# Row sums of q in wide matmuls, with the two half rows joined on ScalarE and VectorE, in an attention and feed-forward kernel

## The chip, the cores and the metric

The kernel runs on one core of a Trainium2 chip. The metric is the device time of one execution in microseconds (us).

Engines: PE is TensorE (PEld its weight loads), DVE is VectorE, ACT is ScalarE, POOL is GpSimd. A load here is a DMA that POOL issues (part 6 of the page lists the loads of k, q and v under POOLq); the profile gives DMA time as a share of 16 DMA engines.

## The reference, cut to what matters

```python
def _attn_ref(q, k, v, tau):                       # B, N, C = 4, 6016, 256
    qn = q / (np.linalg.norm(q, axis=1, keepdims=True) + 1e-06)
    kn = k / (np.linalg.norm(k, axis=1, keepdims=True) + 1e-06)
    s = kn.transpose(0, 2, 1) @ qn / tau           # 256 x 256 per batch
    a = softmax(s)                                 # shortened
    return v @ a
# then a SwiGLU feed-forward over all 24064 rows: (silu(x @ w_gate) * (x @ w_val)) @ w_out
```

The norms are sums of squares over the 6016 rows, for each of the 256 columns. Batch 0 has to be done before the long stretch of dense matmuls can start. Only batch 0's norm of q is touched by the change.

## The kernel before: the parts concerned

q of batch 0 has 47 tiles of 128 rows, taken in 24 pairs. ACT or DVE squares a pair; for pairs 0 to 17 PE sums the squares over the partitions with a matrix of ones, into one row of 256 (`first_row_sums`). The row is copied (`first_row_copy`) and turned into two columns by four PE passes (`first_cols`). The squares of the last pairs are added to these columns directly (`first_col_sums`). The logarithm and exponentials follow.

```python
def first_row_sums(b, t, which, sq, t_last):       # which: 1 for k, 0 for q
    if t == 0:
        ss_new = psum_gv.tile([P, 1 + which, C], FP32, tag="gv"[which])
        state[b, "ss", which] = ss_new
    pm = pairs[t][1]
    ss = state[b, "ss", which]
    if which == 1:                                  # k: one matmul of 512 per pair
        nc.tensor.matmul(ss[:, :pm, :], ones_bf, sq[:, :pm, :], start=(t == 0),
                         stop=(t == t_last), skip_group_check=True)
        return
    for s in range(pm):                             # q: two matmuls of 256 into one row
        nc.tensor.matmul(ss[:, 0, :], ones_bf, sq[:, s, :], start=(t == 0 and s == 0),
                         stop=(t == t_last and s == pm - 1))

def first_row_copy(b):
    row = work.tile([1, C], FP32, tag="row")
    nc.vector.tensor_copy(row, state[b, "ss", 0][0:1, 0, :])
    state[b, "row"] = row
# ...
def keep_warm(n):                                   # dummy matmuls
    ps = psum_o.tile([P, 2, C], FP32, tag="o")
    for _ in range(n):
        nc.tensor.matmul(ps, ones_bf, warm_bf, start=True, stop=True)
# ... order of the loads, all issued by POOL:
#     k, q, then v_sb, then the first two column blocks of w_gate and w_val, ...
# ... in first_softmax, after the column sums:
    rs = psum_m.tile([P, CH], FP32, tag="misc")
    keep_warm(1)
    row_eps(rs)
    transpose_first_v()                             # PE transposes v_sb
    keep_warm(2)
# ... the last pairs of q:
first_row_copy(0)
waiting = []
for n, g in enumerate(range(G_COLS, NQ - 1)):
    ts = range(qgroups[g][0] // 2, (qgroups[g + 1][0] if n < 2 else NS + 1) // 2)
    sqs = [(t, first_square(0, t, 0, on_dve=(t % 2 == 1))) for t in ts]
    for t in ts:
        gemm1_pair(0, t)
    if n == 0:
        first_cols(0)
        keep_warm(1)
    # ... column sums of the group before
```

## Time and profile before

| what | value | read from |
|---|---|---|
| time, first three executions | 809.76, 809.77, 812.23 us | timings |
| span of the profiled one | 808.0 us | page |
| PE busy | 790.9 us, 98% | page, part 1 |
| PE from 35.4 us on | without a hole but 0.10 us at 40.3 and two of 0.07 | table of stretches, PE's timeline |
| start of the dense stretch | first v tile lands at 35.32 | chain of waits |
| first matmul of the output product (o_new) | 52.88 us | PE's timeline |

The page and its views are shown in the prediction below. To read them: busy time is a sum over the whole program; the table of stretches says where PE has holes; the chain of waits, followed back from the end, says which event started the dense stretch. The last row of the table is a ruler: nothing but dense PE work lies between the start of the feed-forward and that matmul, so the time at which it starts tells how late the dense stretch began, holes up to there included.

### The profile page before, as it was taken

Reading aid. Unit: us, or ns where it says so; the run is one execution under the profiler, and the core shown is the slowest. Engines: PE = TensorE matmul, PEld = TensorE weight load, DVE = VectorE, ACT = ScalarE, POOL = GpSimd, SP = SyncE. Lnnn points to the kernel's source line nnn. Section 1 sums busy time; section 2 is a strip of 40 time slices with the busy share of each in tenths; the row PEclk is TensorE's granted clock in tenths of the full one; section 3 lists DMA queues with packets and bytes.
Section 4 is the critical chain, followed back from the end, with each engine's and each line's share of the span. In section 5 each row is a group of like instructions: output and inputs, shape, how many; then the busy total and the mean of one; then the engine's idle time right before and its main releaser. Section 6 shows DMA issues by size and latency. Waiting matters only on the chain.

```text
span 808.0 us, 11840 instructions
## 1 busy us (share of the span) xinstructions
PE 790.9 (98%) x3916; PEld 381.3 (47%) x3916; DVE 554.1 (69%) x856; ACT 454.3 (56%) x802; POOL 249.3 (31%) x299
## 2 busy tenths in 40 slices
PE   4999999999999999999999999999999999999998
PEld 1644444444454444444454444444445444444446
DVE  3777878758667878766766877766866665665654
ACT  3666666555556666555555656555555555555553
POOL 3415887331104786332010768610000000000000
PEclk9999999999999999999999999999999999999999
DMA  8995999899897795877995687556645755555443
GB/s 90 144 158 90 179 158 173 154 114 148 167 147 159 144 154 122 165 122 167 158 175 121 117 157 151 131 131 161 127 118 131 135 133 131 129 145 133 115 112 98
DMA packets 203132, 112.40 MB, mean 139 GB/s; under 512 B 151376, under 2 KB 190160, under 8 KB 202320
## 3 DMA queue, kind: packets, MB, share of 16 engines
q1 hardware_dynamic: 185456, 84.55, 43.7%
q0 software_dynamic: 17472, 27.01, 30.2%
q8 instruction: 30, 0.49, 0.3%
q14 instruction: 30, 0.25, 0.1%
q10 hardware_dynamic: 144, 0.10, 0.0%
HBM read 79.06 MB, written 60.48 MB: 173 GB/s over the span
## 4 chain that ended last, share of the span: by engine, by line
PE 95%; DMA 4%; POOL 0%; issue 0%; DVE 0%; POOLq 0%
PE g_ps L466 30%; PE v_ps L466 30%; PE o_new L507 29%; PE ps L433 2%; DMA q_sb<-in_q_dram 2%; PE kq_new L171 2%; DMA v_sb<-in_v_dram 1%; PE o_new L560 1%; PE last_ps L584 0%; POOL k_sb L114 0%; PE unit_ps L433 0%; PE kq_new L176 0%; PE vt_ps L150 0%; POOL q_sb L114 0%; PE ps L423 0%
## 5 line engine op out<-in xcount | busy, mean ns | idle before, releaser
L476 DVE TENSOR_TENSOR sv<-silu,v_ps 128x512 bf16<-128x512 bf16 (+1 forms) x576 | 386.2, 672 | 214.4 <-ACT silu L472 212.2
L472 ACT ACTIVATE silu<-g_ps 128x512 bf16<-128x512 f32 (+1 forms) x576 | 339.1, 589 | 292.2 <-PE g_ps L466 273.1
L466 PE MATMUL g_ps<-vT,Wg 128*128 128x512 bf16 (+1 forms) x1128 | 330.6, 375 | 0.0
L466 PE MATMUL v_ps<-vT,Wv 128*128 128x512 bf16 (+1 forms) x1128 | 330.4, 374 | 0.0
L507 PE MATMUL o_new<-sv,w_out_sb 128*128 128x512 bf16 (+1 forms) x1104 | 324.5, 376 | 0.0
L466 PEld LDWEIGHTS <-Wv 128*128 128x128 bf16 x1152 | 112.7, 98 | 130.9 <-issue 0.4
L311 POOL TENSOR_TENSOR acc_new<-acc_new,sq 128x512 f32<-128x512 f32 x135 | 157.2, 1164 | 52.3 <-DVE sq L301 36.9
L466 PEld LDWEIGHTS <-Wg 128*128 128x128 bf16 x1152 | 111.3, 98 | 125.7
L507 PEld LDWEIGHTS <-w_out_sb 128*128 128x128 bf16 x1104 | 108.0, 98 | 126.4
L129 POOL DMA_DIRECT2D vb_new<-in_v_dram x47 | 24.2, 515 | 241.5 <-DMA vT<-vb_new 241.0
L517 DVE COPY pl<-o_new 128x512 uint16<-128x512 uint16 (+1 forms) x92 | 62.5, 679 | 14.1 <-ACT pl L516 14.1
L301 DVE TENSOR_TENSOR sq<-q_sb 128x512 bf16<-128x512 fp8e5 x72 | 65.1, 904 | 0.0
L516 ACT COPY pl<-o_new 128x512 uint16<-128x512 uint16 (+1 forms) x92 | 53.1, 577 | 19.6 <-PE o_new L507 19.6
L302 ACT ACTIVATE sq<-k_sb 128x512 bf16<-128x512 fp8e5 x72 | 44.2, 614 | 0.0
L114 POOL DMA_DIRECT2D q_sb<-in_q_dram x45 | 25.4, 566 | 15.3 <-DMA k_sb<-in_k_dram 11.3
L171 PE MATMUL kq_new<-k_sb,q_sb 128*128 128x512 fp8e5 x184 | 28.3, 294 | 0.6 <-DMA q_sb<-in_q_dram 0.6
L171 PEld LDWEIGHTS <-q_sb 128*128 128x256 fp8e5 x184 | 21.1, 136 | 5.0 <-DMA q_sb<-in_q_dram 1.2
L378 POOL TENSOR_SCALAR den<-th 128x512 f32<-128x512 f32 x3 | 1.8, 615 | 66.8 <-ACT th L377 49.8
L114 POOL DMA_DIRECT2D k_sb<-in_k_dram x39 | 21.5, 551 | 1.0 <-POOLq L782 0.8
L346 POOL TENSOR_TENSOR inv<-inv,half 64x8 f32<-64x8 f32 x3 | 5.0, 1665 | 53.3 <-DVE inv L344 53.3
L200 PE MATMUL ss_new<-sq,ones_bf 128*128 128x512 bf16 (+1 forms) x24 | 9.2, 538 | 12.0 <-ACT sq L188 12.0
L306 POOL TENSOR_TENSOR acc_new<-sq 128x512 f32<-128x512 bf16 x3 | 3.5, 1151 | 45.9 <-DVE sq L301 45.9
(94 smaller groups left out, 211.9 us busy)
## 6 DMA issues: line engine op xcount, KB each, us to landing
rows<-pl SPq DMA_DIRECT2D x86, 256.0 KB, 2.5
out_dram<-ot_new SPq DMA_DIRECT2D x43, 512.0 KB, 3.8
vb_new<-in_v_dram POOLq DMA_DIRECT2D x43, 256.0 KB, 4.8
q_sb<-in_q_dram POOLq DMA_DIRECT2D x36, 128.0 KB, 6.5
k_sb<-in_k_dram POOLq DMA_DIRECT2D x33, 128.0 KB, 7.3
ot_new<-rows SPq DMA_TRANSPOSE x92, 3.6
rows<-pl SPq DMA_DIRECT2D x6, 192.0 KB, 2.4
out_dram<-ot_new SPq DMA_DIRECT2D x3, 384.0 KB, 7.1
```

Of the source, the lines that this page charges most:

```text
L114: nc.gpsimd.dma_start(out=dst[:, gs:gs + gm, :], in_=src[b].rearrange("(p s) c -> p s c", s=NS)[:, gs:gs + gm, :])
L129: nc.gpsimd.dma_start(out=vb[:mv, :].rearrange("(p s) c -> p (s c)", s=cm), in_=v[b, cs * P:cs * P + mv, :].rearrange("(p s) c -> p (s c)" ...
L171: nc.tensor.matmul(kq[:, jh, :], q_sb[:, ps:ps + 2, js], k_sb[:, ps:ps + 2, :], start=(t == 0 and jh == 0), stop=last, perf_mode=DR, skip_ ...
L301: nc.vector.tensor_mul(sq[:, :pm, 0, :], q_sb[:, ps:ps + pm, :], q_sb[:, ps:ps + pm, :])
L302: nc.scalar.activation(sq[:, :pm, 1, :], k_sb[:, ps:ps + pm, :], ACT.Square)
L311: nc.gpsimd.tensor_tensor(out=acc, in0=acc, in1=sq[:, s, :, :], op=ALU.add)
L466: nc.tensor.matmul(dst[:, :mv], W[:, kk, fs], vT[:, kk, :mv], start=(kk == 0), stop=(kk == CH - 1))
L472: nc.scalar.activation(silu[:, :mv], g_ps[:, :mv], ACT.Silu)
L476: nc.vector.tensor_mul(sv[:, f, :mv], silu[:, :mv], v_ps[:, :mv])
L507: nc.tensor.matmul(self.o_ps[h][:, :self.mv], w_out_sb[:, f, h * P:(h + 1) * P], self.sv[:, f, :self.mv], start=(f == 0), stop=(f == FH - 1))
L516: nc.scalar.copy(pl[:, 0, :self.mv], halves[:, 0, :self.mv])
L517: nc.vector.tensor_copy(pl[:, 1, :self.mv], halves[:, 1, :self.mv])
```

## The change

The intent, as the diff tells it: q's sums use matmuls of 512 as k's do, which halves their number; the even and odd tiles then lie side by side in two half rows, and these are joined by an ACT copy and a DVE add. The join is put after the squares of the next group, and one dummy matmul goes.

```diff
@@ first_row_sums
-            ss_new = psum_gv.tile([P, 1 + which, C], FP32, tag="gv"[which])
+            ss_new = psum_gv.tile([P, 2, C], FP32, tag="gv"[which])
             state[b, "ss", which] = ss_new
         pm = pairs[t][1]
-        ss = state[b, "ss", which]
-        if which == 1:
-            nc.tensor.matmul(ss[:, :pm, :], ones_bf, sq[:, :pm, :], start=(t == 0),
-                             stop=(t == t_last), skip_group_check=True)
-            return
-        for s in range(pm):
-            nc.tensor.matmul(ss[:, 0, :], ones_bf, sq[:, s, :], start=(t == 0 and s == 0),
-                             stop=(t == t_last and s == pm - 1))
+        nc.tensor.matmul(state[b, "ss", which][:, :pm, :], ones_bf, sq[:, :pm, :],
+                         start=(t == 0), stop=(t == t_last), skip_group_check=True)
@@ first_row_copy
+        ss = state[b, "ss", 0]
         row = work.tile([1, C], FP32, tag="row")
-        nc.vector.tensor_copy(row, state[b, "ss", 0][0:1, 0, :])
+        nc.scalar.copy(row, ss[0:1, 0, :])
+        nc.vector.tensor_add(row, row, ss[0:1, 1, :])
@@ first_softmax
-        keep_warm(1)
         row_eps(rs)
@@ the last pairs of q
-    first_row_copy(0)
     waiting = []
...
         sqs = [(t, first_square(0, t, 0, on_dve=(t % 2 == 1))) for t in ts]
+        if n == 0:
+            first_row_copy(0)
```

## The prediction

> **What bounds the kernel now.** I read the page first, then the busy time by stretches, then the chain of waits in order of time, then the timelines of PE, ACT and DVE between 30 and 41 us, because the diff touches only that part of the program.

> The page's first line gives busy time by engine, and the table of stretches gives, after each stretch's length, the busy time of PE, PEld, DVE, ACT and POOL (number of instructions), the granted clock, the DMA share and GB/s:

> ```profile
> PE 790.9 (98%) x3916; PEld 381.3 (47%) x3916; DVE 554.1 (69%) x856; ACT 454.3 (56%) x802; POOL 249.3 (31%) x299
> ...
> 31.10:35.40 4.30, 3.53 (x43) 2.64 (x42) 3.11 (x8) 2.40 (x6) 2.58 (x4) 1.00 1.28 170
> 35.40:40.40 5.00, 5.00 (x41) 3.27 (x42) 4.02 (x10) 3.71 (x7) 4.09 (x6) 1.00 1.23 205
> 40.40:803.00 762.60, 762.60 (x3716) 363.62 (x3715) 529.88 (x805) 432.69 (x764) 232.51 (x265) 1.00 0.73 141
> ```

> From 35.4 us on PE is busy without a hole; before it, PE has holes. So a change in the first 35 us counts only if it moves the moment from which PE runs without a hole, and then one for one up to the end. The chain of waits says what sets that moment:

> ```profile
> 4.16 19.14 DMA q_sb<-in_q_dram
> 23.59 11.73 DMA v_sb<-in_v_dram
> 35.37 0.62 PE vt_ps L150 x8
> 35.99 0.43 PE ps L423 x2
> ```

> It is a load: the first v tile is issued at 23.59, lands at 35.32, and PE transposes it at once. Nothing that the diff edits stands before 35.37 in this chain. The q work (row sums, row copy, column sums, norm, exponentials) runs beside the load, and what matters is how much later it may end.

> The timelines of DVE and of ACT show the q work (start, length; in brackets the idle time before and what ended it):

> ```profile
> 31.13 0.41 DVE L209 COPY row<-ss_new 1x256 f32<-1x256 f32 x1 [0.63 <-PE ss_new L204]
> 31.47 1.27 DVE L185 TENSOR_TENSOR sq<-q_sb 128x512 bf16<-128x512 fp8e5 x2
> ...
> 34.88 0.40 DVE L259 TENSOR_TENSOR s_f<-kq_new,ink 128x256 f32<-128x256 f32 x1
> 36.03 0.76 DVE L157 COPY vT_new<-vt_ps 128x512 bf16<-128x512 bf16 x2 [0.74 <-PE vt_ps L150]
> ```

> ```profile
> 30.83 0.63 ACT L188 ACTIVATE sq<-q_sb 128x512 bf16<-128x512 fp8e5 x1 [0.57 <-DMA q_sb<-in_q_dram]
> 32.05 0.63 ACT L188 ACTIVATE sq<-q_sb 128x512 bf16<-128x512 fp8e5 x1 [0.58 <-DMA q_sb<-in_q_dram]
> 33.13 0.63 ACT L188 ACTIVATE sq<-q_sb 128x512 bf16<-128x512 fp8e5 x1 [0.46 <-PE cols L227]
> 34.16 0.17 ACT L233 ACTIVATE inq<-cols 128x2 f32<-128x2 f32 x1 [0.40 <-PE cols L227]
> ...
> 35.00 0.91 ACT L270 ACTIVATE exT<-s_f,inq 128x256 bf16<-128x256 f32 x2 [0.44 <-DVE inq L256]
> ```

> PE's timeline around the consumers, and its one later hole:

> ```profile
> 31.59 0.60 PE L217 MATMUL cols<-ones_f,row 1*128 1x1 f32 x4
> ...
> 33.98 0.38 PE L423 MATMUL ps<-warm_bf,ones_bf 128*128 128x512 bf16 x1
> ...
> 36.26 0.19 PE L276 MATMUL rs<-ones_bf,exT 128*128 128x1 bf16 x2
> ...
> 36.53 0.19 PE L276 MATMUL rs<-ones_bf,exT 128*128 128x1 bf16 x2
> ...
> 39.83 0.59 PE L466 MATMUL g_ps<-vT_new,Wg 128*128 128x512 bf16 x2
> 40.36 0.59 PE L433 MATMUL ps<-w_gate_sb,exT 128*128 128x512 bf16 x2
> ```

> The two exponentials end at 35.51 and 35.91, and PE takes them at 36.26 and 36.53: the q path has about 0.7 us of slack for the first and 0.6 us for the second. At 39.83 + 2 x 0.216 = 40.26 PE would be free for the next matmul, which starts at 40.36, when w_gate_sb has landed (40.32 in the trace): a hole of 0.10 us. After it I find only two holes above 0.03 us, 0.07 us each.

> [...] matmuls of 256 start 0.109 us apart and those of 512 0.216, so one wide one saves 2 x 109 - 216 = 2 ns. [...] The trace has the second exponential starting 0.09 us before the first ends, and its two loads at 1283 ns. [...] DVE's square at 31.47 had its data from 30.73 on and stood behind the row copy. [...]

> **The change part by part.**
> (1) Row sums. Pairs 0 to 17 take part: 36 matmuls of 256 become 18 of 512; with the dummy, the instruction order of the changed kernel has 38 PE rows fewer (19 matmuls, 19 weight loads). At 2 ns a pair that is 0.04 us of PE time, all of it before 31.1 us, where PE waits for q's loads (idle there, 11.10 - 10.31 = 0.8 us). Worth nothing at the end.
> (2) Row copy. Before: the sums end at 31.10, DVE copies 31.13 to 31.54, PE's cols matmuls start at 31.59. After, by the order on each engine: ACT first does the square of the next group (30.83 to 31.46), then the copy, then DVE adds. Cost of the ACT copy of 1x256 from PSUM: copies of 128x192 and 128x512 take 319 and 585 ns, so 0.83 ns an element, and 256 come to 372 ns. With an overlap of up to 0.09 it starts at 31.37 to 31.46 and ends at 31.74 to 31.84. Then a hop of 0.035 (ACT to DVE, as from 34.56 to 34.60) and the add, for which ink's add of the same width in the trace took 0.42: 32.20 to 32.29. Then 0.055 to PE (as from 31.54 to 31.59): cols start at 32.25 to 32.35. That is **0.66 to 0.76 us later**, say 0.70.
> (3) What follows on the q path. cols, its dummy, the next products, the column sums of pairs 18 and 19 (which free the buffer of ACT's square at 33.13), that square, its column sums, the logarithm at 34.16, and exT at 35.00 hang together without a wait for a load, so all move by 0.70. exT's halves then end at 36.21 and 36.61.
> (4) Against the v path, which stays: PE is ready for the first half at 36.26 and gets it at 36.21 + 0.05, just in time. It is ready for the second half at 36.53 and gets it at about 36.66: **0.13 us later**, and everything after on PE with it.
> (5) The hole at 40.26: the weight load doesn't depend on the change, so 0.10 of the 0.13 goes into that wait. Left: about **0.03 us**; with the delay at 0.66 to 0.76, 0.0 to 0.1.
> (6) The dummy taken out, at 33.98: PE waits after it until 35.32 anyway. Worth nothing on the path; with (3) it lies where the later column sums now come.
> Sum: 809.77 + 0.03 to 0.1, and I put it at 809.85.

> **The rivals.**
> (a) It gets slower by more. If the copy and the add take longer than I say, or the transfer of the second half costs more, each 0.1 us goes through from here on, since the slack is used up: 810.0 to 810.4. Against: all durations are read from the same trace. A table load for the copy would bring 1.28 us, so about 811; but ACT's instruction order in the changed kernel shows a plain copy with no load.
> (b) It gets faster, because PE has fewer instructions and DVE's square of the next group now comes before the join, 0.63 us earlier. If PE's work until 35.3 set the start, 0.04 us plus the dummy's 0.216 would be gained: 809.5. Against: the chain of waits goes through the v load, and the square that gets earlier (pair 19) isn't used until after the cols matmuls.
> (c) The loads themselves shift. A shorter PE program is fetched a little differently, and the DMA engines are full until 40 us (share 1.23 to 1.28). A landing of v 0.2 us earlier or later moves the end by as much: 809.5 to 810.0. Nothing in the profile says which way.
> (d) PE drops to half its clock in the hole before 35.3. Against: the hole was 0.9 us at a granted clock of 1.00, and it gets shorter.

> **Range and chances.** The mechanism gives 809.8 to 809.9; rivals (a) and (c) widen it to some 809.4 to 810.4. Besides, one of the three timings before was 812.23 against 809.76 and 809.77, for no reason the diff touches; if two of three fall so, the median is there. So the range is 809.3 to 812.3. Two per cent is 16 us, twenty times more than anything here: same 0.99, and 0.005 for either side.

> **What would show each step.** Right: cols matmuls of the row at about 32.3 instead of 31.59; an ACT copy of about 0.37 us and a DVE add of about 0.42 us ahead of it; exT from about 35.7; v's landing within 0.1 us of 35.32 after the start and still in the chain; PE's row sums of exT at about 36.26 and 36.65 with a small hole between; the wait for w_gate_sb near 40.3 gone or nearly gone; the busy time and holes after 41 us as before. Wrong: the chain running through the q path by far more than 0.13 us, the v load landing elsewhere, or a span that moves by more than 0.3 us with the same landing.

The sum is 809.77 us plus 0.03 to 0.1, put at 809.85, and the 2 ns a pair, the overlap of 0.09 us and the 1283 ns (of each of ACT's two table loads) are read from the trace of the kernel before.

## The result, and the profile after

The changed kernel took 810.24, 810.76, 809.71 and 809.84 us: median 810.04. The kernel before has a median of 809.78 over four. A ratio here is the mean time of one kernel's fast runs over that of the other's of the same rounds, so not quite the ratio of the medians that are quoted. It is 0.9997, 95% interval 0.9977 to 1.0017: the same. The predicted time was 809.85.

The time is as predicted, but the trace took another way there. The page's first line and the table of stretches of the changed kernel:

```profile
PE 790.4 (98%) x3897; PEld 379.7 (47%) x3897; DVE 553.9 (69%) x856; ACT 454.8 (56%) x803; POOL 249.3 (31%) x299
...
31.10:35.40 4.30, 3.84 (x51) 3.24 (x50) 2.37 (x8) 2.14 (x6) 3.47 (x6) 1.00 1.29 170
35.40:40.40 5.00, 4.32 (x32) 2.32 (x30) 3.78 (x11) 3.77 (x7) 3.02 (x5) 1.00 1.23 205
40.40:803.00 762.60, 762.60 (x3714) 363.40 (x3712) 530.40 (x806) 433.36 (x765) 232.54 (x265) 1.00 0.74 140
```

The nineteen matmuls are gone (3916 to 3897), and from 40.4 us on PE is as dense as before. But between 35.4 and 40.4 it now has 0.68 us of holes, where it had none. The chain of waits of the changed kernel up to there:

```profile
5.75 23.57 DMA q_sb<-in_q_dram
...
29.62 8.21 DMA w_gate_sb<-in_moe_w_gate_dram
...
37.88 0.61 PE ps L427 x4
```

The load that starts the dense stretch is no longer v_sb but the second block of w_gate_sb, issued at 29.62 and landed at 37.83; before, the same block had landed at 37.12. And v_sb, issued at 23.42, landed at 34.06, 1.26 us earlier than before. The view of tile v_sb says the same from its issue on (11.7 before):

```profile
DMA to landing us min/median/max: 10.6/10.6/10.6
```

The timelines of DVE and then of ACT show the join:

```profile
30.65 0.69 DVE L185 TENSOR_TENSOR sq<-q_sb 128x512 bf16<-128x512 fp8e5 x1 [0.16 <-DMA q_sb<-in_q_dram]
31.64 0.41 DVE L204 TENSOR_TENSOR row<-row,ss_new 1x256 f32<-1x256 f32 x1 [0.29 <-ACT row L203]
```

```profile
31.24 0.36 ACT L203 COPY row<-ss_new 1x256 f32<-1x256 f32 x1
...
35.51 0.91 ACT L264 ACTIVATE exT<-s_f,inq 128x256 bf16<-128x256 f32 x2 [0.44 <-DVE inq L251]
```

PE's timeline:

```profile
32.10 0.60 PE L212 MATMUL cols<-ones_f,row 1*128 1x1 f32 x4 [0.46 <-DVE row L204]
...
36.07 0.20 PE L270 MATMUL rs<-ones_bf,exT 128*128 128x1 bf16 x2 [0.15 <-ACT exT L264]
...
36.47 0.20 PE L270 MATMUL rs<-ones_bf,exT 128*128 128x1 bf16 x2
...
37.88 0.61 PE L427 MATMUL ps<-w_gate_sb,exT 128*128 128x256 bf16 x4 [0.53 <-DMA w_gate_sb<-in_moe_w_gate_dram]
```

The join is there, with the durations foreseen: copy 0.36, add 0.41, cols at 32.10 instead of 31.59. The q path ends 0.51 us later (exT at 35.51 for 35.00). Since v came early, PE waits for exT at 36.07 and 36.47, gets both about as early as before, and then stands still until w_gate_sb is there: 0.53 us by the bracket of that line, and 0.69 if one counts from where the matmul before it has streamed its columns (this second way is used for holes below). In this execution the first o_new matmul starts at 53.44, 0.56 us later than before.

The span is only 0.34 us longer (808.32 against 807.98), because the end of the program gives 0.22 us back. DVE's last copy, before and then after:

```profile
804.49 0.23 DVE L592 COPY last_sb<-last_ps 128x64 f32<-128x64 f32 x1 [3.05 <-PE last_ps L584]
```

```profile
805.05 0.22 DVE L586 COPY last_sb<-last_ps 128x64 f32<-128x64 f32 x1 [3.04 <-PE last_ps L578]
```

From its start to the end of the span it is 3.49 us before and 3.27 after. Over all traces it is 3.49 in six (the two of the kernel before, narrow_join, before_nodummy, before_warm, warm_pad78) and 3.26 to 3.29 in the other eight. It goes with the kernel; no run tests why.

**What moved the loads.** The table of DMA queues for a short stretch gives, per queue, packets, MB, and the time of the packets as a share of 16 engines' time. First the kernel before from 33.0 to 34.2 us:

```profile
q0 software_dynamic: 290, 0.22, 117.3%
q8 instruction: 1, 0.02, 4.9%
```

Then the changed kernel from 35.6 to 36.8 us:

```profile
q0 software_dynamic: 282, 0.37, 174.7%
q8 instruction: 1, 0.02, 4.9%
```

Queue 8 carries what the profile calls instruction, which I read as a fetch of instructions: one packet of 16384 bytes, whose time is 4.9% of 16 x 1.2 us, or 0.95 us. In the trace of before there are 30 such fetches. They start after 240, 459, 719, 989 rows of PE's program (matmuls and weight loads) and so on, one per 254 rows on average. In the kernel before, the first comes at 33.17 us, just when v_sb is being moved. In the changed kernel, whose PE program is 38 rows shorter, it comes at 35.75, when v_sb is through and w_gate_sb's second block is under way. The idea to test is that the fetch makes one of the 16 engines late, and so the load that has a share there.

### The profile page after: what moved, and what is told of

It is laid out like the page before. It is cut to its first block, busy times and chain, and to the rows that moved or that the text cites. A ratio compares the mean times of both kernels' runs of the same rounds, so it can differ in the third digit from the quotient of the medians.

```text
span 808.3 us, 11799 instructions
## 1 busy us (share of the span) xinstructions
PE 790.4 (98%) x3897; PEld 379.7 (47%) x3897; DVE 553.9 (69%) x856; ACT 454.8 (56%) x803; POOL 249.3 (31%) x299
## 4 chain that ended last, share of the span: by engine, by line
PE 95%; DMA 4%; POOL 1%; issue 0%; DVE 0%; POOLq 0%
PE g_ps L460 30%; PE v_ps L460 30%; PE o_new L501 29%; DMA q_sb<-in_q_dram 3%; PE ps L427 2%; PE kq_new L171 2%; DMA w_gate_sb<-in_moe_w_gate_dram 1%; PE o_new L554 1%; POOL q_sb L114 0%; PE last_ps L578 0%; POOL k_sb L114 0%; PE kq_new L176 0%; POOL identf masks.py:199 0%; PE rs L399 0%; POOL identf masks.py:197 0%
## 5 line engine op out<-in xcount | busy, mean ns | idle before, releaser
L466 ACT ACTIVATE silu<-g_ps 128x512 bf16<-128x512 f32 (+1 forms) x576 | 339.2, 589 | 293.1 <-PE g_ps L460 274.0
L305 POOL TENSOR_TENSOR acc_new<-acc_new,sq 128x512 f32<-128x512 f32 x135 | 157.2, 1164 | 52.3 <-DVE sq L295 36.9
L197 PE MATMUL ss_new<-sq,ones_bf 128*128 128x512 bf16 (+1 forms) x42 | 14.5, 459 | 13.4 <-ACT sq L188 13.4
```

The lines of the kernel that those rows point to most:

```text
L305: nc.gpsimd.tensor_tensor(out=acc, in0=acc, in1=sq[:, s, :, :], op=ALU.add)
L466: nc.scalar.activation(silu[:, :mv], g_ps[:, :mv], ACT.Silu)
```

## The experiments

Three theories were put to the test. **A:** the instruction fetch decides which load is late, and the change moves the fetch. **B:** the join's cost is hidden in the slack of the q path, as predicted. **C:** the dummies matter, because PE's clock falls when PE does too little. Each run was timed in five rounds (warm_pad78 in six), beside the kernel before on the same chip. Line numbers are those of each kernel.

### Both kernels once more

No edit.

> The kernel before, unchanged, timed and traced once more: how far the landings of the loads and the time move by themselves. Theory (the loads set the start of the dense PE stretch and they land differently from run to run): the landing of v_sb or of w_gate_sb moves by 0.3 us or more against the first trace (35.32 and about 37.1), and the time spreads over 809.7 to 810.8 as that of the changed kernel did. Rival (the landings moved because of the change): v_sb lands at 35.2 to 35.5 again and the time is 809.76 to 809.79.

> The changed kernel, unchanged, once more. Theory (loads, chance): v_sb and w_gate_sb land elsewhere than at 34.0 and 37.83; the ratio to the kernel before is 0.9995 to 1.0008. Rival (the change moves the loads): they land at about 34.0 and 37.8 again, and the time is 0.2 to 0.5 us above that of before.

before_again took 809.62 to 810.28 us, median 809.86. v_sb landed at 35.35, w_gate_sb's second block at 37.14, the fetch came at 33.2: the first trace again, within 0.03 us. after_again took 809.65 to 811.07, median 810.23, ratio 0.9998 (0.9986 to 1.0011). v_sb was under way for 10.7 us again, the fetch came at 36.1, w_gate_sb's second block landed at 38.10. So the landings belong to the kernel, not to chance: here my theory (chance) lost and its rival won. The times scatter all the same, and before_again shows one source: in its trace PE once stands still for 0.53 us at 189 us, waiting for a product on DVE, which the first trace does not have.

The trace of after_again has something that neither first trace has. The table of stretches, with the granted clock as the third number from the end:

```profile
32.00:35.40 3.40, 2.94 (x39) 2.58 (x41) 1.86 (x4) 1.60 (x4) 2.55 (x4) 1.00 1.32 189
35.40:38.80 3.40, 3.40 (x23) 2.27 (x21) 2.07 (x7) 1.78 (x5) 2.28 (x4) 0.50 1.23 208
38.80:42.20 3.40, 3.35 (x21) 1.89 (x20) 3.04 (x7) 2.85 (x5) 1.20 (x3) 1.00 1.23 204
```

PE ran at half clock from 35.4 to 38.8 us. The first o_new matmul comes at 54.26 instead of 53.44, and this is the slowest of the five (811.07). That is theory C's ground.

### The q path later by eight copies, in both kernels

```diff
         # first_row_copy, after the row is there
+        for n in range(8):
+            late = work.tile([1, C], FP32, tag="late%d" % (n % 2))
+            nc.vector.tensor_copy(late, row)
+            row = late
         state[b, "row"] = row
```

> The kernel before with eight more copies of the joined row, one after another on VectorE, before the cols matmuls read it: the q path comes about 8 x 0.34 = 2.7 us later (an estimate from the 0.30 us of the 256 wide SBUF operation in the trace and a hop of 0.035). Theory (q path has 0.6 us of slack behind the loads and 0.1 us of a later wait for weights): plus 1.7 to 2.2 us. Rival 1 (the q path is far from binding, the loads hide it all): plus 0 to 0.3. Rival 2 (no slack): plus 2.7.

> The changed kernel with the same eight copies. Here the q path binds in both kernels, so the difference to before_late8 is what the join costs on the path. Theory: the end of the sums to the cols matmuls took 0.49 us in the trace before and 0.89 in the one after, so plus 0.4 us against before_late8 (0.3 to 0.7). Rival (the join is free because the wide matmuls end sooner): within 0.15 us of before_late8.

before_late8 took 814.24 to 815.94 us, median 814.64, ratio to before 1.0055; after_late8 814.86 to 815.45, median 815.02, ratio 1.0057. The copies cost what was expected (cols at 34.34 in place of 31.49 in before_again, 2.85 us), but the time rose by some 4.5 us in place of 1.7 to 2.2. The trace of before_late8, by stretches:

```profile
32.20:35.60 3.40, 1.26 (x10) 1.09 (x12) 3.11 (x8) 0.34 (x1) 1.85 (x4) 1.00 1.31 196
35.60:39.00 3.40, 3.40 (x39) 2.65 (x39) 1.67 (x5) 1.73 (x5) 3.40 (x5) 0.50 1.22 208
39.00:42.40 3.40, 3.40 (x20) 2.16 (x19) 1.94 (x6) 1.60 (x4) 0.69 (x2) 0.50 1.24 204
```

PE did little for 3.4 us (busy 1.26) and then had half clock for 6.8. after_late8 has the same from 36.9 to 43.8. The first o_new matmul of before_late8 came at 57.58 for 52.88, 4.70 us later. So the added delay came twice, once as itself and once through the clock. As a measure of the slack the pair failed: what it was to show is swamped. It does rule out that the loads hide any lateness of the q path. The join's cost cannot be read from it either: the means are 814.91 and 815.08, a difference within the scatter.

### The changed kernel with as many PE rows as before

```diff
+    pad_ps = psum_o.tile([P, 2, C], FP32, tag="o")
+    for _ in range(19):
+        nc.tensor.matmul(pad_ps[:, 0, 0:1], ones_bf, warm_bf[:, 0:1], start=True, stop=True)
     for g, which, gl in order:
```

These are one-column matmuls at the start, while PE waits for k.

> The changed kernel with 19 one-column matmuls (38 PE rows with their weight loads) put at the start, while PE waits for the first k load, so that PE's program is as long as before and its first instruction fetch comes at the same row of the rest. Theory (the fetch of 16 KB, one packet of 0.95 us on one of the DMA engines, delays whichever load lies behind it, and the shorter PE program moved it from 33.2 to 35.8 us): the fetch is back at 33.0 to 33.5, v_sb lands 11.5 to 12 us after its issue (35.2 to 35.7), the second load of w_gate_sb at 37.0 to 37.3 instead of 37.8 to 38.1. Rival (something else of the change moves the loads): v_sb lands 10.6 us after its issue as in the changed kernel. Time within 0.3 us of before.

The fetch came at 32.6 us. v_sb landed at 35.35, 11.6 us after its issue and no longer 10.6. The fetch was 0.6 us earlier than in the kernel before, and so it also met a load that I had not named: the last of q, which landed 13.28 us after its issue (11.85 in before), at 34.62. The chain of waits of after_pad19 runs through just that one:

```profile
21.34 13.28 DMA q_sb<-in_q_dram
...
34.67 0.39 PE kq_new L176 x2
```

The median was 811.14 (809.61 to 811.61), ratio 1.0008 (0.9995 to 1.0021), with half clock from 35.9 to 39.3 us in the trace. The loads came out as theory A says, but for the fetch, 0.4 us earlier than expected, and w_gate_sb's second block, which at 37.45 is 0.15 us past its range; the time did not come within 0.3 us of before.

### The same with 100 PE rows

The edit is the same with 50 for 19.

> The changed kernel with 50 such matmuls (100 PE rows) at the start: the fetch moves to about 26 to 30 us, in the middle of q's loads, and the second one past 41 us. Theory A (a fetch delays only what is in flight when it comes, the engine catches up): v_sb lands 10.4 to 10.8 us after its issue and w_gate_sb's second load at 36.9 to 37.2, so neither is late, and PE's first g_ps matmul comes at about 37.5, set by the q path; time 0.1 us below before, hardly to be seen. Theory B (one engine stays behind for the rest of the loads): v_sb and the weights are all about a microsecond late, and time is 0.2 to 1 us above before.

The fetch came at 27.4 us. The load of q then under way was late: issued at 5.24, it landed at 29.47 instead of the changed kernel's 28.06. The next one landed at 29.96, only 0.5 us after it, and v_sb 10.7 us after its issue, w_gate_sb's second block at 36.76. Here, then, only the load that met the fetch is late, as this expectation's A says against its variant (B there), by which all later loads are late.

That does not carry over to a fetch among the last loads. The loads follow the landing of k's first tile, which moves from trace to trace (8.79 us in the first trace of the changed kernel, 9.35 here), so I count from it. In after_late8, whose fetch comes after these loads (39.1 us), v_sb and the four weight loads behind it land at 25.3, 25.9, 26.6, 27.3 and 28.0; in the kernel before, with the fetch at 33.2, at 26.4, 26.8, 27.5, 28.2 and 28.8. There all five are late by 0.8 us or more, which is the variant.

The q load was not harmless either. The chain of waits of after_pad50 runs through it:

```profile
5.24 24.23 DMA q_sb<-in_q_dram
```

The row sums ended at 32.37 instead of 31.21 (0.56 us of this is the later landing of k, not the fetch), and the median was 810.39, ratio 1.0003 (0.9991 to 1.0016), not 0.1 us below before.

### The kernel before without the dummy

```diff
         rs = psum_m.tile([P, CH], FP32, tag="misc")
-        keep_warm(1)
         row_eps(rs)
```

> The kernel before without the dummy matmul ahead of the eps sums, nothing else. Theory (PE waits there for v_sb anyway): the chain and the landings as before, time within 0.15 us of before (ratio 0.9995 to 1.0008). Rival (the dummy keeps the clock up): more executions with a stretch at half clock after 35 us, each 1 to 2 us longer, so a mean 0.3 us or more above that of before.

Median 809.86 (809.47 to 811.69), ratio 1.0000 (0.9987 to 1.0013): nothing to see in the time. But the landings did not stay. With two PE rows fewer the fetch came at 34.0 instead of 33.2, v_sb landed 10.7 us after its issue, and the first block of w_gate_sb came late, 9.99 us after its issue (8.86 in the changed kernel). The chain of waits of before_nodummy:

```profile
26.09 9.99 DMA w_gate_sb<-in_moe_w_gate_dram
...
36.13 0.38 PE unit_ps L432 x2
```

PE held still 0.43 us for it, and still its first o_new matmul came at 52.60, 0.28 us ahead of before. One of five executions was at 811.69, and the kernel before had one of nine above 811 in these rounds: no sign of an effect of the dummy on the clock, with too few executions to exclude one.

### The join alone

```diff
-            ss_new = psum_gv.tile([P, 1 + which, C], FP32, tag="gv"[which])
+            ss_new = psum_gv.tile([P, 2, C], FP32, tag="gv"[which])
...
         for s in range(pm):
-            nc.tensor.matmul(ss[:, 0, :], ones_bf, sq[:, s, :], start=(t == 0 and s == 0),
-                             stop=(t == t_last and s == pm - 1))
+            nc.tensor.matmul(ss[:, s, :], ones_bf, sq[:, s, :], start=(t == 0 and s == 0),
+                             stop=(t == t_last), skip_group_check=True)
# first_row_copy, its place and its two instructions as in the changed kernel; the dummy stays
```

> The join alone: sums in matmuls of 256 as before, but into two halves of the bank, joined on ScalarE and VectorE after the squares of the next group as in the changed kernel; the dummy stays; PE has as many rows as before. Theory: the fetch comes at about 33.2 and v_sb lands at 35.2 to 35.5 as before; from the end of the sums to the cols matmuls 0.8 to 1.0 us (0.49 before); exT ends at 36.2 to 36.5, so PE takes the second half 0 to 0.2 us later than the 36.53 of before; time 0 to 0.2 us above before. Rival (the join costs nothing at all, it hides): row sums of exT at 36.53 still.

This is the run that shows the join with the loads as they were: the fetch at 33.4, v_sb 11.7 us after its issue. The timeline of PE in narrow_join:

```profile
32.44 0.60 PE L218 MATMUL cols<-ones_f,row 1*128 1x1 f32 x4 [0.68 <-DVE row L210]
...
36.44 0.19 PE L277 MATMUL rs<-ones_bf,exT 128*128 128x1 bf16 x2
36.81 0.20 PE L277 MATMUL rs<-ones_bf,exT 128*128 128x1 bf16 x2
```

From the end of the sums (31.32 in the trace) to cols it took 1.12 us, against 0.50 before: the join costs 0.62 us. PE had v_sb 0.18 us later than in the trace of before, in step with everything else of this execution; its first row sums of exT came 0.18 us later with it, its second ones 0.28. The hole ahead of the second is 0.10 us, and 0.12 with the slower step after it, by the trace. At 40.3 there is no hole for w_gate_sb any more. So of the 0.62 us, 0.12 reach PE, and the hole of before takes up 0.10 of them. The time: median 809.92 (809.71 to 810.01), ratio 0.9996 (0.9983 to 1.0010).

### More and fewer dummies

after_warm is the changed kernel with `keep_warm(2)` ahead of `first_cols(0)` and `keep_warm(1)` ahead of `row_eps(rs)`. before_warm is the kernel before with `keep_warm(1)` ahead of `first_cols(0)` and `keep_warm(2)` in place of 1 ahead of `row_eps(rs)`. after_nowarm is the changed kernel without the `keep_warm(1)` that follows `first_cols(0)`:

```diff
         if n == 0:
             first_cols(0)
-            keep_warm(1)
```

> The changed kernel with two dummy matmuls in PE's wait for the joined row (0.7 to 0.9 us idle) and one ahead of the eps sums, where PE later waits for exT (0.3 us idle). Theory of the clock (the granted clock halves for 3.4 us when PE streamed columns for less than about 0.4 of the 3.4 us before; in the traces so far 0.13, 0.13, 0.27 and 0.35 were followed by half clock and 0.43 and above never): the share rises by 3 x 0.216 / 3.41 = 0.19, no execution has a half-clock stretch after 30 us, and all five times are 809.4 to 810.5, the mean 0.3 to 0.8 us below that of after_again and after_pad19. Rival (the slow executions have another cause): one or two of five at 810.8 to 811.7 as in after_again and after_pad19.

> The kernel before with one dummy in PE's wait for the row (0.33 us idle) and a second one ahead of the eps sums. Theory of the clock: plus 0.13 in share, no half-clock stretch after 30 us, no time above 810.8, where the kernel before has had some of 811.7 to 812.2. Rival: such times again. PE's program grows by four rows, so the fetch of instructions may come at another load than v_sb; by itself that moves the time by up to 0.3 us.

> The changed kernel without the dummy after the cols matmuls too. Theory of the clock: the share falls by 0.06 once more, so most executions (three or more of five) have a stretch at half clock after 30 us, and the median is 811.0 to 812. Rival (dummies don't matter, the loads and the q path do): median 809.6 to 810.4 as the changed kernel.

after_warm: 809.89 to 810.74, median 810.25, ratio 0.9998 (0.9985 to 1.0010). before_warm: 809.84 to 810.39, median 809.95, ratio 0.9994 (0.9982 to 1.0007). after_nowarm: 809.64 to 810.70, median 810.21, ratio 0.9995 (0.9981 to 1.0008). None of the three has half clock after 30 us in its trace.

after_nowarm is a miss: I expected a median of 811 to 812 and it is that of the changed kernel. So taking a dummy away does not make half clock the rule. For the two kernels with more dummies, no execution of ten was above 810.8, as expected (two of after_warm's five were above the 810.5 of its expectation), but the gain in the mean did not come for after_warm (810.32, as after_again's 810.33), and before_warm's mean of 810.03 against 810.52 for before in the same rounds is within the interval. With 8 of 47 executions of the kernel before above 811, five without one prove nothing.

In after_warm the fetch, at 36.3, met the second block of w_val_sb (landed at 38.58): one more place where the fetch can fall. PE stood still for 0.30 us from 40.6 on, for the third block of w_gate_sb (40.89); counted from k's first tile that one is no later than in the first trace of the changed kernel.

### Both lessons together

The kernel before, with before_warm's dummies and the one-column matmuls at the start, 78 of them.

> A version that puts both lessons together: the kernel before (join on VectorE alone), the two more dummies of before_warm, and 78 one-column matmuls (156 PE rows) at the start, so that the first instruction fetch comes at about 22 to 24 us, among q's early loads with time to catch up, and the second one after 40 us. Theory (the fetch delays the load that it meets, and only that one): v_sb lands 10.4 to 10.8 us after its issue, w_gate_sb's second load at 36.6 to 37.2 and its third at 39.8 to 40.4, first g_ps matmul at 37.2 to 37.6 and no half clock after 30 us; times 809.4 to 809.9, all five, so 0.3 us or more under the mean of before in the same rounds. Rival (the early fetch pushes all later loads): v_sb at 11.5 us or more after its issue or q's fourth group a microsecond late, times 810 to 811.

Median 810.33 (810.09 to 812.06), ratio 1.0005 (0.9992 to 1.0018). v_sb landed 10.6 us after its issue and w_gate_sb's second block at 36.92, as expected. The rest was missed: the fetches came at 18.4 and 38.4 us and not where I wanted them, all loads of q landed about 0.6 us later than in the trace of before (the first at 21.49 for 20.87; 0.3 us of this was there before the fetch, in k's first tile), POOL issued v_sb at 24.21 and not 23.59, and the first o_new matmul came at 53.28. Moving the fetch among the early loads only moves the loss. One of the six executions took 812.06, at a mean granted clock of 1.000: with before_warm's dummies in place, an execution was slow without half clock. No version that beats both kernels came out.

### The loads and the fetch, over the traces

| kernel | fetch at | v_sb, issue to landing | late against after_late8, by | first o_new | half clock after 30 us |
|---|---|---|---|---|---|
| before | 33.2 | 11.7 | v_sb 1.0, the four loads behind it 0.8 to 0.9 | 52.88 | none |
| before_again | 33.2 | 11.9 | v_sb 1.2, the next four 1.0 to 1.1 | 52.88 | none |
| narrow_join | 33.4 | 11.7 | v_sb 1.0, the next four 0.7 to 0.5 | 53.08 | none |
| before_warm | 33.1 | 11.8 | v_sb 1.1, the next four 0.9 to 1.0 | 52.97 | none |
| before_nodummy | 34.0 | 10.7 | w_gate_sb's first block 1.1, the next three 0.7 to 0.3 | 52.60 | none |
| after | 35.8 | 10.6 | second blocks: w_gate_sb 1.7, w_val_sb 1.3 | 53.44 | none |
| after_nowarm | 35.7 | 10.7 | second blocks: w_gate_sb 1.5, w_val_sb 1.2 | 53.41 | none |
| after_again | 36.1 | 10.7 | second blocks: w_gate_sb 1.5, w_val_sb 1.2 | 54.26 | 35.4 to 38.8 |
| after_warm | 36.3 | 10.7 | w_val_sb's second block 1.3 | 53.44 | none |
| after_pad19 | 32.6 | 11.6 | q's last load 1.4, v_sb and the next four 0.9 to 1.0 | 54.71 | 35.9 to 39.3 |
| after_pad50 | 27.4 | 10.7 | q's fourth load 0.9 | 53.89 | none |
| before_late8 | 33.2 | 11.8 | v_sb 1.1, the next four 0.9 to 1.0 | 57.58 | 35.6 to 42.4 |
| after_late8 | 39.1 | 10.7 | the measure | 58.46 | 36.9 to 43.8 |
| warm_pad78 | 18.4, 38.4 | 10.6 | q's loads 0.3 to 0.4 | 53.28 | none |

The lateness is in us, counted from the landing of k's first tile, for the loads of q, v_sb, and then the first two blocks of w_gate_sb and w_val_sb, which take turns; single ones of 0.2 or less are left out. Each row is one trace, and k's first tile alone moves by up to 0.56 us between traces: a few tenths in "first o_new" can be that. Whatever the kernel, v_sb takes 11.6 to 11.9 us where the fetch lies at 32.6 to 33.4, and 10.6 to 10.7 otherwise.

## Why the prediction was right

The time, 810.04, lies in the range, and "same" was right, but the way there was not the predicted one, and that the number came so close is in part luck. The step that failed in the changed kernel is the premise of (4), "the v path, which stays": v_sb landed at 34.06 instead of 35.32, and the start of the dense stretch was set by w_gate_sb's second block, at 37.83. The first o_new matmul came 0.56 us later, where 0.0 to 0.1 was predicted. The shorter end of the program, which the prediction did not have, took 0.22 us off again, and the range of 3 us, made for the scatter, would have held either outcome. Point by point:

**(1) Row sums worth nothing.** Right: PE's busy time fell by 0.5 us in all, and nothing of it shows in the time.

**(2) The join, 0.66 to 0.76 us.** The mechanism was right; the size was somewhat less, 0.62 us in narrow_join and also 0.61 in after_again (1.11 us from the end of the sums to cols, against 0.50). In the first trace after it was 0.39: there the sums ended at 31.21, almost when ACT was done with the square, so that the ACT copy waited for nothing but the sums. The two instructions took 361 ns (the ACT copy) and 409 (the DVE add) in the trace of after, against 372 ns and 0.42 us that the prediction had estimated from other copies and another add of the first trace.

**(3) and (4) The slack, and 0.13 us at the second half.** Shown by narrow_join, where the loads are as in the kernel before: a hole of 0.10 to 0.12 us at the very place. In the changed kernel itself this step does not apply as written, because the v path did not stay.

**(5) The wait for weights takes up 0.10 us.** Shown in narrow_join, where the hole at 40.3 is gone. In the changed kernel that load, the third block of w_gate_sb, hardly moved either (40.35 for 40.32). What the sum left out is the block before it, the second: it landed 0.7 us later (37.83 for 37.12) and held PE up for 0.69 us.

**(6) The dummy.** On the path it is worth nothing, as predicted (ratio 1.0000). Through the fetch even its two rows moved which load was late, which I had not seen.

**The rivals.** (a) and (b) did not happen. (c), that a shorter PE program shifts the loads, did, and it is a larger term than the one I built the number on: v_sb 1.1 us earlier, w_gate_sb's block 0.7 us later. I had left its sign and size open. When v_sb is early, PE waits for exT and then for w_gate_sb, so little is won by it. (d), the clock, I turned down because "the hole was 0.9 us at a granted clock of 1.00, and it gets shorter". That argument was wrong: after_again had half clock for 3.4 us, and its first o_new matmul came 0.82 us after that of the same kernel's first trace (k's first tile 0.45 later); after_pad19 had it too.

**What is shown and what is not.** Shown: which loads are late goes with where the instruction fetch falls; adding or taking away PE rows that compute nothing needed moves both. Also shown, in the first traces of the two kernels: the late load is late in one part only. Of the 16 landing signals of v_sb in the trace of before, fifteen came by 34.24 us and one at 35.32; of the 16 of w_gate_sb's second block in the trace of after, fifteen by 36.12 and one at 37.83. Argued only: that this part waits on the very DMA engine that carries the fetch; the traces here do not name the engine of a packet. Why the loads behind are late too after a fetch at 33 us and not after one at 27 stays open.

Half clock goes with the slow executions. The record has the mean granted clock of each execution (of the kernel before, of 43: all but the first four). Of these 43, all seven above 811 us have 0.998 or less, so at least one such stretch (half clock for 3.4 of 808 us takes off 0.002), and none of the 22 at 0.999 or 1.000 is above 810.78. But 14 at 0.998 or less are below 811, and warm_pad78's 812.06 had 1.000, so it is not the only cause. Whether the change makes half clock more frequent stays open: the mean clock was 0.998 or less in seven of nine executions of the changed kernel and in 21 of the 43 of the kernel before, and where in the program it fell is known only for the traces. The nine have a mean of 810.25 us, all forty-seven of the kernel before 810.28.

## What to carry to other kernels

Where loads bound the start of the kernel, as here, saving instructions on another engine gained nothing there (19 matmuls fewer, ratio 0.9997), but it changed when instructions were fetched (35.8 us in place of 33.2), and with the fetch at another place among the loads a different one, and some of those behind it, came late by about a microsecond (v_sb up to 1.2 us, w_gate_sb's second block up to 1.7): look for it in the DMA queues before crediting or blaming the arithmetic. Find out what slack the touched path has against the one that binds, and isolate the step (here the join alone) with the loads unmoved before judging it. Count PE's streaming in the stretch before a dense phase, not only the longest hole, when judging whether the clock will hold (here 0.34 or less of 3.413 us ahead of half clock, 0.375 or more ahead of full clock).
